# Last state sums as row scalings and bf16 adds, and C2 summed by adding DMAs, in a two-branch sequence kernel

## The chip, the cores and the metric

The kernel runs on one core of one Trainium2 chip. The metric is the device time of one execution in microseconds (us); lower is better. The program's own order is written out by hand, step by step, so every engine works through a fixed queue.

## The reference

Two branches read x of 2048 rows by 512 columns, and a gate for each row mixes them. Branch a is a diagonal state space model with 512 complex states, branch b is linear attention with 32 heads of 16 and softmax features.

```python
    h = jnp.zeros_like(Bu[:, 0, :])
    for t in range(L):                       # branch a: 2048 steps
        h = Lam_bar[None, :] * h + Bu[:, t, :]
        hs.append(h)
    y = 2.0 * jnp.einsum("blp,dp->bld", hseq, Cmat).real + x * Dskip[None, None, :]
...
    phi_q = jnp.concatenate([_softmax(pq, axis=-1), _softmax(-pq, axis=-1)], axis=-1)   # branch b
    kv = jnp.einsum("bhsf,bhsd->bhfd", phi_k, v)
    num = jnp.einsum("bhqf,bhfd->bhqd", phi_q, kv)
    den = jnp.einsum("bhqf,bhf->bhq", phi_q, z)[..., None] + 1e-6
    o = num / den                            # then heads joined, @ wo
...
    g = _sigmoid((x * gate_w).sum(-1, keepdims=True))
    return g * a + (1 - g) * b
```

## The kernel before

**States.** The 2048 time steps are stored as eight residues r = 0 to 7 of 256 cells. The complex states stand as eight groups m of 64 states, real parts in one half of the 128 partitions and imaginary parts in the other. `LS[:, m, u]` holds the states of the residues u and u + 4 for u = 0, 1, 2, and `HH[:, m]` those of the residues 3 and 7. Steps `b` and `g` (L645 to L681) compute the inputs of the states and local recurrences on TensorE, `z` a scan over cells, `sa`, `sb` and `H` bring the states of HH up to date.

What is then missing is, for each m and each u, the product of a complex number per state with the states before. It can be added in three ways, and `UNITS` (L61) says which is used where: u = 1 first (names h..), then u = 0 (e..), and last u = 2 (d..), which needs the finished u = 1.

- `by_pe` (second letter p): a matmul with a diagonal matrix into PSUM, then a DVE add from PSUM.
- `by_row` (second letter k): two row scalings into one of four slots in `CT` (real part times the states; imaginary part times the states with both partition halves swapped), then two bf16 adds on DVE. The swapped states lie in `HHs`, which is `CS` used again; `st_X` or `st_X2` copies them there by DMA on SyncE's queue.
- `by_dma` (second letter d): the same two scalings for two m at once, then two DMAs from GpSimd's queue that add into LS.

**C2.** Steps `c0` to `c3` scale the transposed C matrices in `CT` by complex numbers into `CS` and `CT`, and `C` (L696) brings CS by four DMAs into the layout of `C2`, against which the states are multiplied in `y`. Since CT is the scratch of the scalings above and CS that of the swapped states, both must have been read before these start.

**Attention.** `k`, `v`, `q` project tiles of 128 rows. `x`, `n`, `e`, `s` and, for queries, `X`, `N`, `E`, `S` make the softmax features of a group of tiles: largest and smallest value, differences, exponentials on ScalarE (ACT), then sums, and for queries transposes by DMA. `a` accumulates the keys' sums, `Y` brings them from PSUM. `o` makes the output of a tile of rows (a matmul, logarithm and exponential `ld` and `rd` on ACT, the DVE product `on`, L891); `O` transposes `on` of two tiles by DMA on SyncE's queue into `oT`.

**Output.** `y` (L847) accumulates states times C2 in a PSUM bank for each of sixteen tiles; `t` adds `oT` times Wo into the same bank and scales by the gate. Tiles 8 to 11 have a residual `xd` (step `u`) that is added then. The tiles 12 to 15 belong to the residues 2 and 6 and so need all of u = 2. `R` stores two tiles; the last tile is cut into 384 and 128 columns.

**Order.** Each step is a generator, and the string `ORDER` lists in which order they are advanced; `name@banks` gives PSUM banks and `name:D` puts the piece on VectorE (DVE) instead of ACT. All instructions of an engine stand in this order in its queue, and an engine whose next instruction waits does nothing else.

Of the kernel before, what the change touches and what calls it, by code (L numbers as in the profile page):

```python
# [23 lines left out]
ORDER = """
Z@0 Lk Lk Z Z Z B Z Z B Z Z Z Lx Z Z W01@2 Z W00@3 Z B Z W00 Z B W01 W10@1 W00 Lx B W10:D W11@4 Lx W01 Z f0@2 f1@5
T1@1 W11 T0@4 f0:D f1 Lv T1 f2@3 f3@0 Lx Lx T0:D f2 V@2 V k1@5 P k0@4 f3:D P Lx P2 P k0 P2 P2 U P2 k1 P2 U P3 P4 k0
k1 U k2@2 P3 P4 k3@1 n0 v0@5 P4 x0 k5@6 k2 v1@2 Lb Lq n0 i x0 P2 k7@0 v3@4 i V2@3 k3 x0 v0 k5 i n0 i k9@1 x0 v1 i i
Lq x0 n0 Lb k7 M n0 k8@7 k4@0 M k6@2 n1 M Lx w2@6 x1 w0@5 V2 v6@3 x0z Lx n1 x1 v3 n1 L Da Lx Lb Lb x1 Lb Da Lb e0 n1
k4 w3@4 k6 k9 w3 x1 w0 x1 v6 k10@0 n1 k10 s0 x2 k11@2 s0 w1@4 k8 M2 e1 k13@1 k15@3 w1 Db x2 k15 b11@7 U x2 b10@5 k11
b01@0 b20@4 n2 x2 Lc n2 b10 x2 n2 s0 w2 n2 M2 s0 k13 b00@3 n2 M2 g01@5 Da Db x3 g10@1 b30@6 s0 b01 b20 s0 Lc e2 Db  # L30
s1 b31@4 g10 g30@0 n3 b30 s0 c1:D x3 b00 g00@3 s1 g30 k12@6 c0:D b31 g00 g01 k14@2 e2 b11 a0@74 g00 gw a0 g01 g10 n3
q1@1 s1 b21@3 n3 x3 s1 Da s1 x3 g30 v2@0 c0:D k12 n3 s1 q3@6 k14 q0@2 g01 s2 x3 n3 s2 q1 q1 b21 Lc c0:D q2@3 n4
g11@1 x4 e3 g11 g11 q3 v2 g31@0 g01 s1 x4 q3 g20@6 g31 q0 q0 a1 q2 n4 s2 x4 e3 g31 g20 c0 g11 g01 n4 c2 g01 g31 a1
g01 g20 s2 g21@2 x4 q2 g11 s3 Lc g21 c2 g21 g11 s2 v5@3 g01 g21 c1 v5 g31 g21 s2 x4 v4@6 g21 s3 c2:D g31 s3 b40@3
g01 g11 v4 g21 n4 s3 g31 g21 s3 g31 v7@5 b50@6 b40 g21 g31 n4 g11 s2 q6@3 X0 N0 G0 c1 g21 s2 X0 g11 a2 q4@2 c2 g31
q7@0 c1 g11 q6 N0 b50 z0@6 c3 Lo z0 b70@1 v7 a2 q4 s3 z0 q4 q5@5 q7 a2 e4 q6 s3 q7 b70 q5 X0 e4 N0 z0 a2 c3 X0 b71@3
z0 g40@6 X0 b61@1 N0 z0@0 b71 g50@2 b61 g50 g50 q5 z0 z0 b51@5 X1 c3 v10@0 g40 s4 b60@3 z0 sa0@2 g70@1 b51 g61@5 N0
X1 b60 g71@3 s4 g71 g70 v10 g51@0 c3 sa0 X1 g40 sb0@2 Ld s4 s3 N1 g60@6 sb0 N1 s4 g51 g61 g51 N1 E0 E0 C g60 C g70
g51 S0 v11@2 s4 G1 N1 G0 v8@1 g60 Ld S0 g51 H1@6 g61 v11 s4 v8 X1 S0 b41@2 v9@1 g51 H1 S0 s4 hd1 C g51 s4 a3 S0 g71
v9 g41@6 a3 b41 g41 H0@2 g41 a3 a3 hd1 G0 g71 g51 C S0 g71 g61 g41 G1 S0 g71 g61 H0 g41 XX0 g41 q9@2 g61 g71 hd0 G1  # L40
g51 g51 g61 g71 g41 g61 q10@1 X1 g61 XX0 g41 N1 q9 g71 g41 g61 q8@0 g71 g41 S0 hd1 z1@6 q8 q10 z1 S0 z1 q11@3 q9 q11
v13@6 z1 q10 E1 q8 E1 z1 v12@0 XX0 z1@1 X2 N2 v14@2 q14@5 v13 q11 v12 z1 z1 X2 XX0 v15@1 N2 q12@3 z1 v15 hd0 v14 S0
S0 N2 hd1 hd1 hd0 hd1 q14 S1 a4 N2 S1 X2 sa1@0 a4 S1 sa1 a4 q12 a4 sb1@6 S1 q13@0 Y Y sb1 S1 hd0 q15@7 Y X2 H2@6 Y
o0@1 q14 G2 S1 END q15 X2 XX1 y1@5 q15 hd0 q13 q12 S1 o0 o1@3 H3@7 N2 y1 H3 o1 H2 hd0 o3@6 XX1 XX1 o0 q13 o0 o1 E2
E2 o1 N3 S1 XX1 y3@0 hk4 S1 o2@1 y2@4 y0@3 y2 O0 o2 y0 S1 y0 S2 o3 X3 o2 hk6 y1 o3 hk4 hk7 o2 t1 t0 y3 o3 hk7 hk6
y4@1 y2 S2 hk4 hk5 O1 t0 S2 o5@6 X3 S2 y3 hk4 hk7 S2 N3 t1 X3 S1 o4@2 S2 y6@5 hk5 X3 t2 S2 o5 ek0 hk5 hk7 R0 S2 o4
o5 o4 ek0 t3 hk5 hk6 t2 o4 ek3 ek3 o5 t3 o6@2 S2 N3 S2 hk6 X3 N3 o6 o7@6 y5@4 ek0 o7 o6 N3 o6 O2 o7 o7 ek2 ek1 y5 y4
y6 S2 dp5@0 ek1 y4 ek3 y5 dp6@2 o8@6 dp6 dp5 y6 E3 t4 ek2 Ld o9@2 o8 ek0 y7@0 o9 y7 ek2 ek1 o8 t5 o8 o9 ek2 o9 ek1
ek4:D E3 o10@6 t4 y7 o10 O3 o11@2 ek5 S3 t7 ek3 o10 t6 ek6 o11 ek4 o11 O4 y10@1 o10 S3 G2 dp1@6 ek5:D y11@7 t6 t7 t5
o11 ek5 S3 O5 ek7 ek6 ek4 ek5 ek7 S3 dp0@2 ek6 R2 ek7 ek4 y9@0 ek6 ek7 S3 dp7@4 y8@3 dp2@5 S3 dp2 y10 y8 dp3@5 t8  # L50
y11 S3 R1 S3 dp7 dp4@4 G2 dp1 u8 S3 S3 S3 t11 t8 G3 dp0 t10 y9 t9 o13@2 dp3 o13 o12@5 o12 u9 dp4 t9 R3 y14@4 y12@0
u10 o12 G3 y14 o12 o13 o15@5 o13 o15 y12 o15 o14@2 t10 o14 G3 y12 o14 u11 o15 y13@1 O6 y13 t11 y15@56 y15 y13 t12
t13 R4 R5 o14 O7 y14 t14 O8 t12 t13 R6 y15 t14:D R7 t15 t15 t15 R8 t15:D R8
"""
# [20 lines left out]
def kernel(  # L75
# [610 lines left out]
    def st_c(j):  # L686
        scaled(CS[:, 1, j], CT[:, 0, j], csp[:, 1, j:j + 1])
        yield
        scaled(CS[:, 0, j], CT[:, 1, j], csp[:, 2, j:j + 1])
# [3 lines left out]
        VT(out=CS[:, :, j], in0=CS[:, :, j], in1=CT[:, :, j], op=ALU.add)
# [307 lines left out]
```

## Time and profile before

| | us |
|---|---|
| median of 3 runs (lowest, highest) | 151.49 (151.43, 152.28) |
| the profiled execution, its own time | 151.96 |
| its span | 150.2 |
| TensorE (PE) busy | 140.9 |
| VectorE (DVE) busy | 135.1 |
| ScalarE (ACT) busy | 121.9 |
| GpSimd (POOL) busy | 21.4 |

The span is the time from the first to the last instruction of the profiled execution; what lies around it is 1.8 us. The granted TensorE clock was 0.996 over the span. Busy times of different engines overlap. A line such as L735 is that line of the kernel before; in the changed kernel lines are one higher up to L692, and a few higher behind.

### The profile page before, as it was taken

The numbers are of one execution on the slowest core, as the hardware profiler recorded it, in microseconds if no ns is written. First come the engines' busy times: TensorE is split into PE (matmuls) and PEld (weight loads), VectorE is DVE, ScalarE is ACT, GpSimd is POOL, SyncE is SP. The second block draws the span as 40 slices with busy tenths as digits, with TensorE's granted clock in tenths as the row PEclk, the third lists the DMA queues.
The fourth block names the chain that finished last, engine by engine and source line by source line (L and its number), as shares of the span: only waits on it lengthen the run. The fifth ranks groups of instructions, "written<-read, shape, count | busy, mean of one in ns | idle before, by whom it ended". The sixth has DMA issues, their size and how long they took to land.

```text
span 150.2 us, 2835 instructions
## 1 busy us (share of the span) xinstructions
PE 140.9 (94%) x986; PEld 75.2 (50%) x986; DVE 135.1 (90%) x332; ACT 121.9 (81%) x241; POOL 21.4 (14%) x47
## 2 busy tenths in 40 slices
...
GB/s 120 237 265 178 143 230 232 166 180 238 20 0 0 0 0 4 2 0 105 244 74 94 183 142 70 175 186 181 229 181 166 156 65 212 128 214 77 201 82 72
DMA packets 54110, 19.73 MB, mean 131 GB/s; under 512 B 44496, under 2 KB 54096, under 8 KB 54096
## 3 DMA queue, kind: packets, MB, share of 16 engines
...
q14 instruction: 7, 0.06, 0.2%
...
## 4 chain that ended last, share of the span: by engine, by line
PE 55%; DVE 24%; SPq 10%; DMA 7%; issue 1%; ACT 0%; DVEq 0%
PE PS L516 12%; PE PS L860 9%; PE PS L648 9%; PE PS L643 9%; PE PS L916 6%; SPq L236 5%; DMA xT<-in_A_x_dram 4%; DVE on L891 3%; DVE sm L566 3%; SPq L249 3%; DMA oT<-on 3%; PE PS L660 2%; DVE EE L577 2%; DVE EE L616 2%; DVE HH L735 2%; DVE EE L583 2%
## 5 line engine op out<-in xcount | busy, mean ns | idle before, releaser
L516 PE MATMUL PS<-WKV,xT 128*128 128x480 bf16 (+1 forms) x128 | 29.6, 373 | 1.7 <-DMA xT<-in_A_x_dram 1.7
L589 ACT ACTIVATE EE<-EE 128x2048 bf16<-128x2048 bf16 x16 | 30.7, 1944 | 0.0
L516 PEld LDWEIGHTS <-xT 128*128 128x128 bf16 x192 | 18.3, 99 | 20.0 <-DMA xT<-in_A_x_dram 1.8
L860 PE MATMUL PS<-C,LS 128*128 128x512 bf16 (+1 forms) x104 | 23.0, 363 | 0.0
L135 ACT CAST Xq<-PS 128x480 bf16<-128x480 f32 x32 | 17.6, 584 | 1.7 <-PE PS L516 1.7
L916 PE MATMUL PS<-Wo,oT 128*128 128x512 bf16 (+2 forms) x68 | 15.6, 367 | 0.3 <-DMA oT<-on 0.3
L643 PE MATMUL PS<-xT,BT 128*128 128x512 bf16 x64 | 15.7, 379 | 0.0
L648 PE MATMUL PS<-xT,BT 128*128 128x512 bf16 x64 | 15.6, 379 | 0.0
L516 PE MATMUL PS<-Wq,xT 128*128 128x481 bf16 x64 | 15.0, 367 | 0.0
L135 ACT CAST LS<-PS 128x512 bf16<-128x512 f32 x24 | 14.1, 630 | 0.9 <-PE PS L648 0.7
L860 PEld LDWEIGHTS <-LS 128*128 128x128 bf16 x104 | 9.5, 98 | 9.7
L684 POOL DMA_DIRECT2D LS<-CT x4 | 4.9, 1226 | 62.2 <-ACT HH L135 49.6
L922 ACT ACTIVATE ot<-PS,G 128x512 bf16<-128x512 f32 (+1 forms) x11 | 7.2, 670 | 5.8 <-PE PS L916 5.7
L882 ACT ACTIVATE ld<-PS 128x32 f32<-128x32 f32 x16 | 2.8, 197 | 10.2 <-PE PS L877 7.6
L465 ACT ACTIVATE CT<-HH,dgs 128x512 bf16<-128x512 bf16 x15 | 10.7, 718 | 0.2 <-DVE HH L735 0.2
L891 DVE TENSOR_TENSOR on<-PS,rd 128x512 bf16<-128x512 f32 x16 | 10.8, 710 | 0.0
L577 DVE TENSOR_TENSOR EE<-Xq,mx 128x2048 bf16<-128x2048 bf16 (+1 forms) x9 | 10.0, 1107 | 0.8 <-PE PS L633 0.8
L465 ACT ACTIVATE CT<-CS,nsn 128x512 bf16<-128x512 bf16 x15 | 10.5, 725 | 0.0
L583 DVE TENSOR_TENSOR EE<-mn,Xq 128x2048 bf16<-128x2048 bf16 (+1 forms) x9 | 10.0, 1112 | 0.0
L566 DVE TENSOR_TENSOR sm<-EE 128x2048 bf16<-128x2048 bf16 (+1 forms) x9 | 10.0, 1107 | 0.0
L135 ACT CAST vx<-PS 128x512 bf16<-128x512 f32 x16 | 9.9, 633 | 0.1
L604 DVE TENSOR_TENSOR EE<-EE,rc 128x2048 bf16<-128x2048 bf16 x8 | 9.7, 1219 | 0.1
...
## 6 DMA issues: line engine op xcount, KB each, us to landing
out_dram<-ot SPq DMA_DIRECT2D x7, 256.0 KB, 2.4
C<-CS SPq DMA_DIRECT2D x4, 256.0 KB, 4.0
CS<-HH SPq DMA_DIRECT2D x8, 128.0 KB, 3.5
LS<-CT POOLq DMA_DIRECT2D x4, 256.0 KB, 4.5
...
```

What stands on the lines that cost most here:

```text
L135: nc.scalar.copy(out=out_ap, in_=in_ap)
L465: nc.scalar.mul(out=out_ap, in_=in_ap, mul=s_)
L516: MM(out=pt[:], lhsT=xT[:, kt, ti * P:(ti + 1) * P], rhs=W[:, kt, 0:pt.shape[-1]], start=(kt == 0), stop=(kt == KT - 1))
L566: VT(out=dst, in0=cur[:, :, :, 0:n, :], in1=cur[:, :, :, n:2 * n, :], op=op)
L577: VT(out=half(EE, 0), in0=X5, in1=live["mx", p].to_broadcast([P, L, 8, Dh, 4]), op=ALU.subtract)
L583: VT(out=half(live["EE", p], 1), in0=live["mn", p].to_broadcast([P, L, 8, Dh, 4]), in1=X5, op=ALU.subtract)
L589: aexp(out=EE[:, l_:l_ + 2], in_=EE[:, l_:l_ + 2], func=ACT.Exp)
L643: MM(out=pt[:], lhsT=BT[:, m, kt, :], rhs=cells(kt, r), start=(kt == 0), stop=False, skip_group_check=True)
L648: MM(out=pb[:], lhsT=BT[:, m, kt, :], rhs=cells(kt, 2 * pr), start=(kt == 0), stop=(kt == KT - 1))
L860: MM(out=py[:], lhsT=hs[m], rhs=C2[:, m, c:c + w], start=(m == 0), stop=False)
L891: VT(out=live["on", g_][:, u], in0=pn[:, :, :, 0:Dh], in1=rd[:].unsqueeze(3).to_broadcast([P, 2, 16, Dh]), op=ALU.mult)
L916: MM(out=py[:], lhsT=oT[:, g, :], rhs=Wo[:, g, c:c + w], start=False, stop=(g == HG - 1))
```

## The change

The names dp0 to dp7 in `UNITS` become dk0 to dk7: the sums of u = 2 are made by `by_row` instead of `by_pe`. With that the step XX2 comes in, two DMAs that bring the partition halves of `LS[:, :, 1]` swapped into HHs. In `st_c` the DVE sum of CS and CT goes; a new step `A` adds CT into C2 by four adding DMAs on GpSimd's queue after `C` has stored CS there.

```diff
-UNITS = (... (2, 'dp0', 0), (2, 'dp1', 0), (2, 'dp2', 0), (2, 'dp3', 0), (2, 'dp4', 0), (2, 'dp5', 0), (2, 'dp6', 0), (2, 'dp7', 0))
+UNITS = (... (2, 'dk0', 0), (2, 'dk1', 0), (2, 'dk2', 0), (2, 'dk3', 0), (2, 'dk4', 0), (2, 'dk5', 0), (2, 'dk6', 0), (2, 'dk7', 0))
...
         scaled(CT[:, :, j], CT[:, :, j], csp[:, 0, j:j + 1])
         yield
-        VT(out=CS[:, :, j], in0=CS[:, :, j], in1=CT[:, :, j], op=ALU.add)
-        yield
...
+    def st_A():
+        for q, pq_ in ((0, 0), (1, 1), (0, 1), (1, 0)):
+            add_by_dma(C2[q * HS:(q + 1) * HS, pq_::2], CT[pq_ * HS:(pq_ + 1) * HS, 1 - q])
+            yield
```

The list of steps is another one from the first line to the last. Its end, from the transfers XX2 on:

```diff
-o7 o6 N3 o6 O2 o7 o7 ek2 ek1 y5 y4 y6 S2 dp5@0 ek1 y4 ek3 y5 dp6@2 o8@6 dp6 dp5 y6 E3 t4 ek2 Ld o9@2 o8 ek0 y7@0
-...
-t13 R4 R5 o14 O7 y14 t14 O8 t12 t13 R6 y15 t14:D R7 t15 t15 t15 R8 t15:D R8
+o11 ek6 o11 y11 S3 y10@4 G2 S3 y10 o10 S3 XX2 t4 S3 y9@3 o11 y8@6 dk0 S3 S3 XX2 dk2:D O4 dk1 dk1 y8 dk0 y9 t5 R3 dk2
+t8 t9 S3 dk0 O5 dk3 dk1 S3 dk5 dk2 dk0 dk4 dk2 G3 t10 dk6 dk4 G2 S3 dk6 dk5:D t11 dk3 o12@1 u10 S3 dk3 dk4 dk7 dk5
+o12 o12 y12@7 dk6 dk7 dk4 t10 y13@4 dk6 dk7 o12 o13@0 y14@2 o13 o13 dk5 dk7 u11 o13 y14 G3 y12 R2 u8 o14@0 t11 t8
+y14 y13 y13 o14 y12 o14 o14 u9 o15@5 O6 G3 y15@01 R5 y15 o15 O7 o15 t9 t13 t12 o15 R4 t14 y15 O8 t12 t14 t15 t13:D
+t15 R6 t15 R7 t15:D R8 R8
```

At its start the loads Wv (`Lv`) stand ahead of the first x transpose (`Lx`), the loads of B (`Lb`) ahead of the last four, and the transposes of Wq (`Lq`) behind all but one of them; the projections v0 and v2 stand ahead of k0.

More of the change, by code (lines that the diff above doesn't have):

```diff
@@ L24 @@
 ORDER = """
[L25 to L49, printed above, removed]
@@ L50 @@
-o11 ek5 S3 O5 ek7 ek6 ek4 ek5 ek7 S3 dp0@2 ek6 R2 ek7 ek4 y9@0 ek6 ek7 S3 dp7@4 y8@3 dp2@5 S3 dp2 y10 y8 dp3@5 t8
-y11 S3 R1 S3 dp7 dp4@4 G2 dp1 u8 S3 S3 S3 t11 t8 G3 dp0 t10 y9 t9 o13@2 dp3 o13 o12@5 o12 u9 dp4 t9 R3 y14@4 y12@0
-u10 o12 G3 y14 o12 o13 o15@5 o13 o15 y12 o15 o14@2 t10 o14 G3 y12 o14 u11 o15 y13@1 O6 y13 t11 y15@56 y15 y13 t12
-t13 R4 R5 o14 O7 y14 t14 O8 t12 t13 R6 y15 t14:D R7 t15 t15 t15 R8 t15:D R8
+Z@0 Lk Z Z Z Lk B Z Z B Z W01@1 Lx W00@2 B B Z Z Z Z Z B Lx Z W10@3 W11@4 W00 W10 Lv W01 T0@3 Lx Z W11 f2@4 f3@5
@@ new lines @@
+T1@6 W01 f2 W00:D Lx T1 V@1 Lx Z f1@2 f0@7 T0:D V P Z v0@1 Lb f0 v2@0 P f1 f3 P2 P2 P2 k0@2 P2 V2@7 P P2 k1@6 P2 P4
+Lb Lx P4 k1 k0 P3 P3 k3@5 k4@4 P4 k1 k0 i k6@2 i k4 V2 k5@6 k2@4 i k3 M i k7@5 x0 n0 v1@7 Lx v6@3 x0 n0 gw v0 n0 x0
+i x0 k6 M n0 k2 M x0 i U n0 k5 x1 Lx n1 x1 k9@6 n1 k8@4 v1 v3@7 x1 k10@2 k11@1 Lb n1 x1 Lb Lq Lq k7 n1 v2 x1 L b00@0
+n1 k9 M2 b10@6 Da Lx e0 v3 b30@7 n2 x2 x2 n2 x2 k10 b00 s0 g30@0 k11 b20@1 Db e1 n2 b31@2 s0 Db b30 U g00@7 k8 v6 n2
+b20 k12@1 x2 s0 Lc Da g30 x2 s0 M2 n2 b31 U k13@2 g20@3 x3 b10 g20 s0 n3 s1 w2@6 b11@4 e2 U g00 Da x3 n3 k12 k15@1
@@ new lines @@
+s1 n3 x0z e2 v7@5 k13 w1@2 Lc s1 s0 w2:D w0@6 k15 k14@1 g30 g20 b11 w1 w3@3 M2 w0 Lb s1 b01@0 s1 x3 s2 b01 s1 x3
+b21@2 s0 s2 w3 a0@64 a0 Lc g31@0 g00 b21 s2 Db n3 s2 s2 q1@3 q0@2 Da k14 q1 x3 n3 c1 x4 Lc q1 g31 q3@1 c0:D v7 c3
+g31 c3:D v4@7 q0 g01@3 s2 c2:D n4 x4 q3 g21@5 g01 c2:D n4 Lb q3 q2@1 g01 q0 g10@2 v4 n4 s1 x4 c0:D e3 a1 s2 g01 g31
+g01 x4 g21 q2 e3 C g21 a1 g10 g31 q4@7 q2 g10 n4 g31 b40@1 g11@2 c2:D q4 a2 g21 g31 s2 b40 g11 g21 s3 g11 x4 g01 g31
+c3:D g31 q4 g21 g11 g01 Lo X0 n4 N0 b50@1 c1 v5@7 g21 g31 g11 g01 b50 g11 g01 v5 c1:D q10@1 g50@0 a2 a2 a2 X0 g21 G0
@@ new lines @@
+g11 s3 N0 e4 s3 g11 X0 g01 N0 g21 X0 g21 q7@7 q10 g11 s3 g11 G0 b61@3 z0@2 b51@5 q10 z0 z0 g50 q5@2 X0 q7 e4 z0 b61
+q5 g50 s4 b51 s3 b70@1 q6@3 v8@0 N0 q5 z0 z0@5 s4 b60@2 z0 c0 q6 q7 q11@7 z0 N0 X1 g51@5 s4 b60 q6 s3 g60@2 z0 b71@3
+q11 g60 X1 b70 g51 E0 v9@1 v8 g51 sa0@0 C s3 b71 g70@3 E0 q11 X1 N1 s3 s4 g70 sa0 v9 b41@7 S0 g70 a3 g51 A sb0@1
+v10@0 g61@3 g61 A sb0 g60 a3 g61 b41 Ld S0 H1@7 v11@1 H0@2 N1 G1 v10 S0 N1 Ld C S0 g40@0 C G1 s4 A H1 s4 S0 a3 G0
+g40 A g71@7 g71 S0 s4 XX0 v11 H0 g71 X1 hd1 g51 g61 a3 hd1 g41@2 g40 hd0 s4 g41 N1 g51 g71 S0 g41 g51 g61 g71 g41
@@ new lines @@
+g51 g61 q8@0 hd1 g71 g61 g61 g41 X1 XX0 S0 q8 g41 g51 N1 g71 q9@1 g61 g71 S0 XX0 g51 q9 g41 g41:D g71 g41 g71 g61:D
+q8 G1 g41 z1@5 q9 X2 z1 X2 XX0 N2 S0 v14@2 v13@1 v15@7 v12@0 z1 E1 E1 X2 v13 z1 N2 v14 v12 z1 z1@5 N2 z1 Ld S0 X2
+v15 hd1 hd0 N2 q12@3 q14@1 S1 q12 a4 a4 z1 a4 S1 a4 z1 S1 Y q13@7 sa1@5 S1 X2 sa1 q12 hd1 q14 Y q15@0 q15 Y Y sb1@2
+hd0 o3@5 o2@3 hd1 hd0 END sb1 S1 hd0 S1 q15 N2 H2@2 o3 q13 y2@0 XX1 o2 q13 S1 H3@7 o2 o3 H2 y3@2 E2 E2 H3 o2 o3 y1@7
+o0@3 y2 hd0 o1@5 X3 y3 y1 o0 XX1 G2 S1 hk7 o1 X3 o0 hk4 S2 XX1 o0 o1 XX1 y1 y4@3 S2 y2 o1 S2 O1 S1 q14 hk5 hk6 hk7
@@ new lines @@
+y0@4 hk5 S2 t2 hk4 hk4 S1 t2 O0 hk7 y0 y3 t3 hk5 N3 S2 hk4 hk6 o5@0 o4@5 X3 S2 y0 S1 hk7 ek0 hk5 S2 hk6 t3 ek1 o4 t0
+t1 y5@2 o5 S2 o4 hk6 ek0 N3 S2 o5 ek1 t0 o4 t1 N3 y4 ek1 y4 ek3 o5 o6@5 N3 ek2:D ek1 o6 S2 ek2:D ek3 ek0 o6 ek3 o7@0
+X3 S2 ek2 y7@4 ek3 y6@7 o6 o7 o7 ek5 o7 y6 ek7 ek2 y6 o9@5 o8@0 ek0 X3 y7 ek5 o9 N3 ek4:D y5 ek7 o8 ek6:D y7 ek6 ek7
+O2 ek5 y5 t5 o8 ek4 O3 t7 o8 o10@0 R0 o9 R1 E3 ek7 E3 t6 ek5 o10 ek4 t6 o9 t7 ek6 t4 y11@5 o10 o11@6 ek4 dk3 dk1 S3
+o11 ek6 o11 y11 S3 y10@4 G2 S3 y10 o10 S3 XX2 t4 S3 y9@3 o11 y8@6 dk0 S3 S3 XX2 dk2:D O4 dk1 dk1 y8 dk0 y9 t5 R3 dk2
@@ L60 @@
 ZB = 2
-UNITS = ((1, 'hd0', 1), (1, 'hd1', 1), (1, 'hk4', 1), (1, 'hk5', 1), (1, 'hk6', 1), (1, 'hk7', 1), (0, 'ek0', 0), (0, 'ek1', 0), (0, 'ek2', 0), (0, 'ek3', 0), (0, 'ek4', 0), (0, 'ek5', 0), (0, 'ek6', 0), (0, 'ek7', 0), (2, 'dp0', 0), (2, 'dp1', 0), (2, 'dp2', 0), (2, 'dp3', 0), (2, 'dp4', 0), (2, 'dp5', 0), (2, 'dp6', 0), (2, 'dp7', 0))
+UNITS = ((1, 'hd0', 1), (1, 'hd1', 1), (1, 'hk4', 1), (1, 'hk5', 1), (1, 'hk6', 1), (1, 'hk7', 1), (0, 'ek0', 0), (0, 'ek1', 0), (0, 'ek2', 0), (0, 'ek3', 0), (0, 'ek4', 0), (0, 'ek5', 0), (0, 'ek6', 0), (0, 'ek7', 0), (2, 'dk0', 0), (2, 'dk1', 0), (2, 'dk2', 0), (2, 'dk3', 0), (2, 'dk4', 0), (2, 'dk5', 0), (2, 'dk6', 0), (2, 'dk7', 0))
 XLOADS = ((2, 2), (4, 2), (6, 2), (8, 2), (10, 2), (12, 2), (14, 2))
```

2 lines of the change are left out of this document (1 added, 1 removed).

## The prediction

> **What bounds the kernel now.** I read the page's busy times first, then the busy time by stretches of ten microseconds, then the chain that ended last, and then the instructions of VectorE (DVE), ScalarE (ACT) and SyncE's queue in order of time near the end.
>
> ```profile
> PE 140.9 (94%) x986; PEld 75.2 (50%) x986; DVE 135.1 (90%) x332; ACT 121.9 (81%) x241; POOL 21.4 (14%) x47
> ```
> ```profile
> 110.00:120.00 10.00, 9.70 (x88) 5.32 (x84) 10.00 (x21) 9.54 (x20) 0.00 (x0) 1.00 0.97 169
> 120.00:130.00 10.00, 9.76 (x46) 4.46 (x47) 10.00 (x25) 6.47 (x15) 0.00 (x0) 1.00 0.56 120
> 130.00:140.00 10.00, 10.00 (x78) 5.22 (x77) 9.37 (x17) 1.97 (x8) 0.00 (x0) 1.00 0.79 170
> 140.00:150.20 10.20, 6.10 (x50) 3.68 (x47) 1.10 (x2) 1.96 (x3) 0.00 (x0) 0.94 0.37 103
> ```
>
> The columns are the stretch, its length, then PE, PEld, DVE, ACT and POOL busy with their counts. Three engines are full at once up to about 127 us. ACT stops first, DVE next, and PE alone fills the end. The page's 94% for PE flatters it, because matmuls overlap; DVE, at 90% with its idle time at the two ends, is the engine with no room. The last instructions show how the end comes about:
>
> ```profile
> 115.99 4.20 DMA oT<-on
> 120.24 1.90 PE PS L916 x8
> 122.14 0.86 PE PS L860 x4
> 123.00 0.21 PE PS L811
> ```
> ```profile
> 145.91 0.58 ACT ot L922
> ```
> ```profile
> 126.86 0.19 ACT L818 ACTIVATE G<-nge 128x4 f32<-128x4 f32 x1
> 134.09 0.45 ACT L882 ACTIVATE ld<-PS 128x32 f32<-128x32 f32 x2 [7.04 <-PE PS L877]
> ```
> ```profile
> 136.43 0.74 DVE L920 SCALAR_TENSOR_TENSOR ot<-PS,G,xd 128x512 bf16<-128x512 f32 x1
> 137.09 0.17 DVE L822 RECIPROCAL G<-G 128x4 f32<-128x4 f32 x1
> 137.17 0.73 DVE L896 SCALAR_TENSOR_TENSOR xd<-WKV,G,Drow 128x512 f32<-128x512 bf16 x1
> 137.81 0.69 DVE L891 TENSOR_TENSOR on<-PS,rd 128x512 bf16<-128x512 f32 x1
> 138.41 0.74 DVE L920 SCALAR_TENSOR_TENSOR ot<-PS,G,xd 128x512 bf16<-128x512 f32 x1
> 139.07 0.68 DVE L891 TENSOR_TENSOR on<-PS,rd 128x512 bf16<-128x512 f32 x1
> ```
>
> The chain from 120.24 to 145.91 is matmuls without a gap. ACT has done its bulk at 127.05 and then waits 7.04 us. DVE's last product `on` ends at 139.75, and the last output scaling on ACT starts 6.16 us after that. So a change pays by shortening DVE's queue, or by shortening those 6.16 us; ACT may grow at the end, and nowhere else.
>
> **The change, part by part.** I cost an instruction on a full engine by the distance between starts, not by its duration, since neighbours overlap by about 0.1 us.
>
> ```profile
> 115.00 1.32 DVE L735 TENSOR_TENSOR LS<-PS,LS 128x512 bf16<-128x512 f32 x2
> 116.20 0.46 DVE L806 TENSOR_TENSOR LS<-CT 128x512 bf16<-128x512 bf16 x1
> 116.53 0.80 DVE L804 TENSOR_TENSOR CT<-CT,LS 128x512 bf16<-128x512 bf16 x2
> 117.20 0.73 DVE L891 TENSOR_TENSOR on<-PS,rd 128x512 bf16<-128x512 f32 x1
> ```
> ```profile
> 122.06 0.40 DVE L467 TENSOR_SCALAR CT<-CS,nsn 128x512 bf16<-128x512 bf16 x1
> 122.33 0.73 DVE L891 TENSOR_TENSOR on<-PS,rd 128x512 bf16<-128x512 f32 x1
> ```
> ```profile
> 45.73 0.69 DVE L693 TENSOR_TENSOR CS<-CS,CT 128x1024 bf16<-128x1024 bf16 x1
> 46.34 0.29 DVE L566 TENSOR_TENSOR mn<-mn 128x256 bf16<-128x256 bf16 x1
> ```
>
> *DVE.* Removed are the eight adds out of PSUM of dp0 to dp7 (1.20 / 2 = 0.60 each, 4.80) and the four sums of CS and CT in st_c (0.61 each, 2.44). Added are sixteen bf16 adds of dk0 to dk7 (0.33 each, 5.34). The new list also marks other steps for DVE: four more row scalings (six for two; 0.27 each, 1.08), two more 512-wide scalings and one more 1024-wide one in st_c (0.27 each and at most 0.54; I take 0.9 in all), one fold evacuation less (I take the 0.57 of a 480-wide evacuation, between the 0.60 of an add out of PSUM and nothing) and two 64-wide evacuations more (at most 0.3). Sum: -4.80 -2.44 +5.34 +1.08 +0.9 -0.57 +0.3 = -0.2 us. DVE's queue is as long as before: the two halves of the change cancel on the engine that counts.
>
> *PE.* Eight 512-wide matmuls go, 0.21 each as the row of L811 shows: 1.7 us less, most of it in the closing run from 120.24 on, and nothing is added.
>
> *ACT.*
>
> ```profile
> 84.35 3.71 ACT L589 ACTIVATE EE<-EE 128x2048 bf16<-128x2048 bf16 x2
> 87.96 1.55 ACT L135 CAST vx<-PS 128x512 bf16<-128x512 f32 x3
> ```
> ```profile
> 119.65 0.72 ACT L465 ACTIVATE CT<-HH,dgs 128x512 bf16<-128x512 bf16 x1
> 120.26 0.32 ACT L885 ACTIVATE rd<-ld,nge 128x32 f32<-128x32 f32 x1
> ```
> ```profile
> L465 ACT ACTIVATE CS<-CT,csp 128x512 bf16<-128x512 bf16 x5 | 3.8, 761 | 0.0
> L465 ACT ACTIVATE CT<-CT,csp 128x1024 bf16<-128x1024 bf16 x2 | 2.4, 1200 | 0.0
> ```
>
> Fourteen of the sixteen dk scalings run here at 0.61: 8.5. Away go two ek scalings (1.2), two CS scalings and one CT scaling in st_c (their means less the 0.1 of overlap: 2.4), one evacuation more comes than goes (0.5), and two 64-wide ones leave (0.35). Net +5.05 us, so ACT's bulk would end near 132 instead of 127, where before it waited. That is hidden as long as the last dk add is due after about 132.
>
> *The copies.* XX2 puts two more transfers of 256 KB on SyncE's queue, behind the oT transposes of O2 and O3 and the stores R0 and R1, and the swapped dk scalings wait for them; queued behind those on ACT are the remaining dk scalings, the `ld` and `rd` of o12 to o15, and so DVE's last products. A puts four adding transfers on POOL's queue.
>
> ```profile
> C<-CS SPq DMA_DIRECT2D x4, 256.0 KB, 4.0
> CS<-HH SPq DMA_DIRECT2D x8, 128.0 KB, 3.5
> LS<-CT POOLq DMA_DIRECT2D x4, 256.0 KB, 4.5
> ```
> ```profile
> oT<-on SPq DMA_TRANSPOSE x9, 3.1
> ```
> ```profile
> L684 POOL DMA_DIRECT2D LS<-CT x4: 1190/1196/1322, 78.8 to 95.1; - x4
> ```
>
> XX2 can issue once the last ek scaling is done and lands some 5 us later (3.5 and 4.0 us for the copies of 128 and 256 KB, and the second issue). In the new order of ACT, between the last ek scaling and the first swapped dk scaling stand E3's two exponentials (1.80 each, by the starts 84.35 and 87.96), three output scalings, three plain dk scalings and small ones: some 8 us. So I cost XX2 at nothing; bounds are nothing and, if SyncE is as late as at 115.99 with a transpose that took 4.20, 2 us. For A: between the last step of c0 on ACT and hd1's first scaling, which overwrites what A reads, the new order has twenty ACT instructions, among them two exponentials and thirteen evacuations (0.47 each, 87.96 with its three): 10.8 us. Three issues of 1.2 and a landing of 4.5 are 8.1. A costs nothing too, with 2.7 us to spare; without that cover ACT would stand still. C itself no longer waits for the sums and starts sooner.
> The Trainium skill (DMA: Bandwidth & Descriptors, SWDGE vs HWDGE vs iDMA) says that GpSimd writes the rings of its DMAs in state from which DVE's two-port modes lock it out. The four POOL issues of this trace took 1190 to 1322 ns beside a DVE that was nearly full, so it does not show such a hold-up; by the rule A's transfers would start one after another and the time would be that of rival 3.
>
> *The start.* The new list loads Wv before the x transposes and B before Wq, and runs v0 and v2 ahead of k0. PE's one long early wait is this:
>
> ```profile
> 22.57 1.79 PE L516 MATMUL PS<-WKV,xT 128*128 128x480 bf16 x8 [1.65 <-DMA xT<-in_A_x_dram]
> ```
>
> The transposes for k10 and k11 now stand ahead of both Wq transposes, so up to 1.65 us of this wait may go. DVE is full meanwhile, so I count nothing; bounds are a gain of 1.65 and, should the earlier B loads delay k8 and k9 instead, a loss of 1.
>
> *The end.* After the last dk add, DVE still has three `on` (0.60), three `xd` and three `ot` (0.66) and two small ones (0.08) before o15's product is done: 5.9 us. PE has from there two dozen 512-wide matmuls (0.215 each, 5.2), y15 and t15 (2.6), sixteen 128-wide ones and two o steps (1.4): 9.1 us. With DVE's last product at 139.55 the last dk add is at 133.6, PE can be done at 142.8, and o15's way is longer: transpose 3.1, a queue step of 0.1, the 384-wide matmuls 0.67, which is 3.9 after `on` instead of 6.16. That is **the gain: 2.3 us**, because the 1.7 us of diagonal products no longer lie in PE's closing run, and PE no longer ends later than the oT transpose allows.
>
> *Given back.* In the new order DVE has, after the last of N3 (the differences whose exponentials E3 takes), 25 bf16 adds (8.3), eight `on` (4.8), four `xd` and four `ot` (5.3), four row scalings (1.1), G3's sums and products (3.8, an estimate from the 0.33 of a 512-wide and the 0.61 of a 1024-wide add) and small ones (0.3): 23.6 us. So E3 can start at 116.0 and ends at 119.6, and 12.6 us of ACT work (fourteen dk scalings 8.5, four output scalings at the 0.58 of the last one, small ones 1.8) lead to 132.2. Twice ACT must wait for DVE in this stage, for `smf` and for `dl`: 1.1 us by the same sums. With two adds behind the last scaling (0.7) the last dk add ends at 134.0, 0.4 late. For the four slots of CT that dk4 to dk7 must wait for I add 0.3; bounds are nothing and 5.4, below.
>
> Sum against the profiled execution of 151.96 us: -0.2 -2.3 +0.4 +0.3 = -1.8, 150.2. That execution is 0.47 over the median of 151.49, so against the median: **149.7 us**, 1.2% less. A measurement of this kernel tells about 1% from no change, which puts the bounds at 149.98 and 153.0.
>
> **The rivals.** (1) *The gain is given back as idle time of DVE.* In the list of before, DVE stood idle for only about 2 us between 8 and 139.75; a list searched anew need not be as dense. For: three full engines, with ACT's queue 5 us longer. Against: DVE's load is unchanged. With 1 to 3 us more idle it ends at 150.7 to 152.7; I take 151.5. (2) *Slower: the slots.* by_row has four slots for eight m, so dk4 to dk7 start only after the second adds of dk0 to dk3 on DVE. If every reuse costs a full trip (0.71 for the scaling, 0.46 for each of two adds, 0.6 for an `on` in front: 2.2 for each of four, against 8.4 us for the stage without waits, 4.9 of them for the first four), the stage lasts 13.8, 5.4 more, and the time is 155.1. It decides the sign from 3.3 us of such waits on. For: in the new order o12's product and two `xd` stand among these adds. Against: dk1 and dk3 run ahead, so the trips overlap. (3) *A lands late and holds hd1 on ACT.* If the four adds go one after another at the 4.5 of their landing, they need 18 us where 10.8 are covered: 7.2 us on a full ACT, 156.9; it would take issues much longer than the 1.2 us of the rows, or adds that don't overlap, and the trace of before shows neither. The rule named with A would bring this about. (4) *The start's 1.65 us count as well:* 148.0.
>
> **How the numbers follow.** Forecast 0.46 (its own range 148.8 to 150.6, six parts in seven of it under 149.98), rival 1 0.26, rival 2 0.18, rival 3 0.05, rival 4 0.05. Faster: 0.40 + 0.05 = 0.45. Within 1%: 0.06 + 0.26 = 0.32. Slower: 0.23. The range takes in rival 4, the forecast, rival 1 and the lower part of rival 2: 148.0 to 153.4.
>
> **What would show it.** Right: DVE full to about 139.5 with its last `on` there; ACT's bulk ending near 132; the last output scaling on ACT starting about 4 us after the last `on`, with the oT transpose as its releaser; PE with no wait for the adds of the dk steps beyond a few tenths. Wrong: waits of ACT for DVE adds at the dk scalings of over 3 us in sum (rival 2); a wait of ACT's hd1 scaling for LS or C transfers (rival 3); SyncE holding XX2 so that the swapped scalings wait; DVE idle for more than 3 us between 10 and 139 (rival 1). If DVE's last product comes well before 139, my price list for DVE is wrong.

## The result, and the profile after

The changed kernel takes 149.98 us (median of 4 runs, 149.85 to 150.24) beside 151.55 for the kernel before (151.43 to 152.28): ratio 0.9889, 95% interval 0.9866 to 0.9912, 1.1% less. The forecast was 149.7 with a range of 148.0 to 153.4. Run once more, it had 150.33 (ratio 0.9883, 0.9847 to 0.9920). The profiled execution of after has 149.94 us and a span of 148.2; that of before had 151.96 and 150.2.

First the page's busy times, then the last stretches of 10 us (stretch, length, PE, PEld, DVE, ACT, POOL busy, granted clock, DMA share, GB/s):

```profile
PE 139.1 (94%) x962; PEld 73.8 (50%) x978; DVE 135.5 (91%) x344; ACT 127.8 (86%) x249; POOL 27.3 (18%) x51
```
```profile
110.00:120.00 10.00, 9.52 (x88) 5.33 (x88) 10.00 (x25) 9.73 (x20) 0.00 (x0) 1.00 1.08 216
120.00:130.00 10.00, 9.89 (x53) 4.47 (x52) 10.00 (x26) 9.82 (x20) 0.00 (x0) 1.00 1.00 182
130.00:140.00 10.00, 9.86 (x86) 5.46 (x86) 9.94 (x22) 5.47 (x15) 0.00 (x0) 1.00 0.73 161
140.00:150.20 10.20, 4.66 (x33) 2.60 (x32) 1.94 (x4) 1.96 (x3) 0.00 (x0) 0.96 0.37 103
```

ACT now works to 134 instead of 127, DVE has as much to do as before, and only PE has less. Take PE's account alone: before, 150.2 of span less 140.9 busy leaves 9.3 us in which PE stood idle; after, 148.2 less 139.1 leaves 9.1. By this account PE's shorter work is nearly the whole gain of this execution. The account says where the time went, and not what allowed it: before_thin below takes 1.4 us off PE in the old list and gains nothing. The end of the chain that ended last, and the last rows of ACT and DVE:

```profile
126.91 5.27 DMA phT<-EE
132.71 1.67 PE PS L864 x7
134.64 2.59 PE PS L864 x12
139.28 1.75 PE PS L864 x16
141.07 2.54 PE PS L920 x11
```
```profile
132.23 0.43 PE L881 MATMUL PS<-KVm,phT 128*128 128x68 bf16 x8
```
```profile
133.24 0.71 ACT L466 ACTIVATE CT<-CS,nsn 128x512 bf16<-128x512 bf16 x1
144.52 0.58 ACT L926 ACTIVATE ot<-PS,G 128x384 bf16<-128x384 f32 x1 [0.18 <-PE PS L920]
```
```profile
133.98 0.75 DVE L810 TENSOR_TENSOR LS<-CT 128x512 bf16<-128x512 bf16 x2
140.16 0.68 DVE L895 TENSOR_TENSOR on<-PS,rd 128x512 bf16<-128x512 f32 x1
```

The transposes of the last query features (phT) are done at 132.18, the product o12 that reads them starts at 132.23, and from there PE works to the end. The two rows for the kernel before, on PE and in SyncE's queue:

```profile
133.63 0.67 PE L877 MATMUL PS<-KVm,phT 128*128 128x68 bf16 x16
```
```profile
127.91 4.81 SPq L620 DMA_TRANSPOSE phT<-EE  x2
```

Before, o12 started at 133.63, 0.9 us behind the end of its transposes and 12.28 us ahead of the last scaling on ACT (145.91). Now it is 12.29 us ahead of it (144.52). So the question is what lets o12 start 1.4 us earlier.

### The profile page after: what moved, and what is told of

Same layout as the page of the kernel before. It is cut to its first block, busy times and chain, and to the rows that moved or that the text cites. A ratio compares the mean times of both kernels' runs of the same rounds, so it can differ in the third digit from the quotient of the medians.

```text
span 148.2 us, 2857 instructions
## 1 busy us (share of the span) xinstructions
PE 139.1 (94%) x962; PEld 73.8 (50%) x978; DVE 135.5 (91%) x344; ACT 127.8 (86%) x249; POOL 27.3 (18%) x51
## 4 chain that ended last, share of the span: by engine, by line
PE 60%; DVE 22%; ACT 6%; DMA 5%; issue 4%; DVEq 0%; SPq 0%
PE PS L517 23%; PE PS L644 9%; PE PS L649 9%; PE PS L864 5%; DMA phT<-EE 4%; DVE on L895 3%; DVE sm L567 3%; ACT EE L590 2%; PE PS L920 2%; PE PS L634 2%; DVE LS L810 2%; DVE CT L808 2%; DVE mn L567 2%; DVE HH L739 2%; DVE mx L567 2%
## 5 line engine op out<-in xcount | busy, mean ns | idle before, releaser
L517 PE MATMUL PS<-WKV,xT 128*128 128x480 bf16 (+1 forms) x125 | 28.7, 372 | 0.2
L864 PE MATMUL PS<-C,LS 128*128 128x512 bf16 (+1 forms) x100 | 21.8, 362 | 0.3
L136 ACT CAST Xq<-PS 128x480 bf16<-128x480 f32 x32 | 18.4, 586 | 1.2 <-PE PS L517 1.2
L644 PE MATMUL PS<-xT,BT 128*128 128x512 bf16 x64 | 16.1, 379 | 0.1
L649 PE MATMUL PS<-xT,BT 128*128 128x512 bf16 x64 | 15.8, 380 | 0.1
L517 PE MATMUL PS<-Wq,xT 128*128 128x481 bf16 x64 | 15.5, 368 | 0.1
L466 ACT ACTIVATE CT<-CS,nsn 128x512 bf16<-128x512 bf16 x22 | 15.2, 715 | 0.0
L920 PE MATMUL PS<-Wo,oT 128*128 128x512 bf16 (+2 forms) x67 | 15.1, 366 | 0.1
L136 ACT CAST vx<-PS 128x512 bf16<-128x512 f32 x16 | 9.3, 604 | 0.5 <-PE PS L517 0.4
L920 PEld LDWEIGHTS <-oT 128*128 128x128 bf16 x68 | 6.2, 98 | 6.5 <-DMA oT<-on 0.5
L649 PEld LDWEIGHTS <-BT 128*128 128x128 bf16 x64 | 6.1, 99 | 6.4
L644 PEld LDWEIGHTS <-BT 128*128 128x128 bf16 x64 | 6.1, 98 | 6.4
```

Source lines behind the costliest of these rows:

```text
L136: nc.scalar.copy(out=out_ap, in_=in_ap)
L466: nc.scalar.mul(out=out_ap, in_=in_ap, mul=s_)
L517: MM(out=pt[:], lhsT=xT[:, kt, ti * P:(ti + 1) * P], rhs=W[:, kt, 0:pt.shape[-1]], start=(kt == 0), stop=(kt == KT - 1))
L644: MM(out=pt[:], lhsT=BT[:, m, kt, :], rhs=cells(kt, r), start=(kt == 0), stop=False, skip_group_check=True)
L649: MM(out=pb[:], lhsT=BT[:, m, kt, :], rhs=cells(kt, 2 * pr), start=(kt == 0), stop=(kt == KT - 1))
L864: MM(out=py[:], lhsT=hs[m], rhs=C2[:, m, c:c + w], start=(m == 0), stop=False)
```

## The experiments

The table holds five times from the profiled execution of each kernel: DVE's first product of the parameters (ssm_par from vec), the first differences of N3 on DVE (before's list has them at another place), o12 on PE, the last output scaling on ACT, and the last time less the first. The ratio is that of the timed runs to the kernel before.

| kernel | first product | N3 | o12 | last scaling | last less first | ratio (95%) |
|---|---|---|---|---|---|---|
| before | 8.83 | 110.73 | 133.63 | 145.91 | 137.1 | 1 |
| after | 9.05 | 114.95 | 132.23 | 144.52 | 135.5 | 0.9889 (0.9866, 0.9912) |
| again | 10.05 | 115.94 | 132.97 | 145.26 | 135.2 | 0.9883 (0.9847, 0.9920) |
| c2_dve | 9.04 | 116.76 | 134.08 | 146.37 | 137.3 | 1.0055 (1.0029, 1.0081) |
| dp_back | 9.03 | 114.91 | 133.69 | 146.78 | 137.8 | 1.0075 (1.0040, 1.0111) |
| pe_refill | 9.98 | 116.19 | 134.96 | 147.24 | 137.3 | 0.9992 (0.9964, 1.0021) |
| before_A | 8.96 | 112.33 | 134.74 | 147.01 | 138.1 | 1.0066 (1.0043, 1.0089) |
| before_thin | 8.94 | 110.76 | 132.92 | 145.28 | 136.3 | 0.9999 (0.9986, 1.0011) |
| no_dk | 9.34 | 115.21 | 132.24 | 144.52 | 135.2 | 0.9906 (0.9880, 0.9932) |
| start | 9.19 | 115.31 | 132.34 | 144.64 | 135.5 | 0.9925 (0.9893, 0.9957) |
| start_v | 10.25 | 116.56 | 133.69 | 145.98 | 135.7 | 0.9952 (0.9925, 0.9979) |
| no_ek | 8.89 | 112.47 | 132.16 | 144.44 | 135.6 | 0.9917 (0.9889, 0.9945) |
| pe_less | 9.05 | 114.96 | 132.42 | 144.71 | 135.7 | 0.9919 (0.9888, 0.9949) |
| no_ek_less | 10.63 | 114.24 | 132.76 | 145.78 | 135.2 | 0.9896 (0.9862, 0.9930) |

The theory at the outset was the prediction's: DVE's queue is full and sets the end, PE follows it. Its rivals were that only one half of the change gains, or that PE alone sets the end.

**c2_dve: the sums of C2 back on DVE.**

```diff
         scaled(CT[:, :, j], CT[:, :, j], csp[:, 0, j:j + 1])
         yield
+        VT(out=CS[:, :, j], in0=CS[:, :, j], in1=CT[:, :, j], op=ALU.add)
+        yield
...
 in the list: the sum behind the third step of each c; the four A become the four C, the early C go
```

> Base: the changed kernel, 149.98. Undone: the adding DMAs A; the four sums of CS and CT are DVE adds again (0.61 us each), C stores after them. Theory of the queues (DVE is full from 13 to 140 us, and its length is passed on to the end): DVE is 2.4 us longer, 152.4 (151.6 to 152.6). Rival (ACT and PE set the pace where these sums stand, at 45 to 65 us, and DVE has room for them): 150.0 to 150.4.

152.77 us, ratio 1.0055: 2.5 us more than after (0.0166 of 151.5), as the theory of the queues had it. The table shows how it runs through: N3 1.81 later, o12 1.85, the end 1.85. Rows of DVE and PE of c2_dve, in order of time, and PE's sum of waits from 48 to 72 us (us in all, times, longest):

```profile
53.82 0.69 DVE L693 TENSOR_TENSOR CS<-CS,CT 128x1024 bf16<-128x1024 bf16 x1
54.43 0.15 DVE L550 TENSOR_SCALAR nge<-PS 128x1 f32<-128x1 f32 x1
```
```profile
54.63 1.02 PE L516 MATMUL PS<-WKV,xT 128*128 128x512 bf16 x4 [1.02 <-DVE nge L550]
```
```profile
PE PS L516 <- DVE nge L550: 1.3, 2, 1.0
```

The sum stands ahead of the small `nge`, which frees the PSUM bank that PE wants, and PE waits 1.3 us, where after has no such wait and PE stands idle for 0.16 us in all in the same stretch. At this place a late DVE makes PE late, and nothing behind makes it good.

**before_A: the adding DMAs alone, in the list of before.** The edit is that of the change in `st_c` and its step A; in the old list the four C now stand together behind the second step of c3, the last of the c steps, and the four A behind its third.

> Base: the kernel before, 151.5. Done alone: C2 is summed by four adding DMAs on GpSimd's queue, and the four DVE sums go; list otherwise as before. Theory of the queues: DVE is 2.4 us shorter; ACT, full at the same time with 2.4 us idle between 40 and 127, passes on only part, 150.0 (149.2 to 150.6). Rival (PE's closing run sets the end of the kernel before, whatever DVE does): 151.3 to 151.6.

152.90 us, ratio 1.0066, slower than before by 1.0: neither theory nor rival had that. From its GpSimd and ACT rows, and its SyncE queue:

```profile
67.33 3.22 POOL L684 DMA_DIRECT2D C<-CT  x3 [38.08 <-DMA C<-CS]
```
```profile
77.61 0.72 ACT L465 ACTIVATE CT<-HH,dgs 128x512 bf16<-128x512 bf16 x1 [1.92 <-DMA C<-CT]
```
```profile
72.04 10.29 SPq L777 DMA_DIRECT2D CS<-HH  x4
```

In the old order A is issued 3 us later than in the new one (64.34). ACT waits 1.92 us for A's transfers before hd1, and SyncE's four copies of the swapped states, which start 3.6 us earlier than before's (75.63, over 5.33 us), end 1.4 us later. This is the prediction's rival 3, in the other list: a landing, not an issue, holds hd1. So A alone, put into the old list like this, costs more than it saves; in the new list, which moves the c steps ahead, ACT did not wait for it.

**dp_back: u = 2 by diagonal products again, in the list of after.**

```diff
-UNITS = (... (2, 'dk0', 0), ... (2, 'dk7', 0))
+UNITS = (... (2, 'dp0', 0), ... (2, 'dp7', 0))
...
 in the list: a matmul and an add of each dp stand at places where dk steps stood; XX2 goes
```

> Base: the changed kernel, 149.98. Undone: dk0 to dk7; the sums of u = 2 are matmuls with the diagonal and DVE adds out of PSUM again, at the places in the list where the dk steps stood, and XX2 goes. Theory of the queues: DVE is 1.1 us shorter, PE's closing run 1.7 longer, so about 0.6 slower, 150.6 (150.0 to 151.2). Rival 1 (the row scalings are the gain): 151.3 or more. Rival 2 (the gain comes from C2 and from the list, and the dk steps cost): 149.0 to 149.6.

153.13 us, ratio 1.0075, 2.8 us more than after: above the theory's range and in that of rival 1. The places of the dp steps are mine, not searched, so this is an upper bound of what the row scalings are worth. The waits from 119 us on:

```profile
DVE LS L738 <- PE PS L814: 2.2, 2, 1.6
PE PS L863 <- DVE ot L923: 0.3, 1, 0.3
```

DVE now waits 2.2 us for the products, and o12 starts 1.46 later. Undone singly, the two halves cost 2.5 and 2.8 us, together more than the whole gain of 1.6: they are not two savings that add. Both undone at once in the new list was not run, so how much of the gain the new order would bring without the change stays open.

**pe_refill: 1.7 us of empty matmuls put back on PE, ahead of o12, in after.**

```diff
+    def st_Q():
+        pq_ = bank([P, 512], F32, "pq_")
+        while True:
+            MM(out=pq_[:], lhsT=Sw[:], rhs=C2[:, 0, :], start=True, stop=True)
+            yield
...
 in the list: eight Q at the places of eight dk steps
```

> Base: the changed kernel, 149.98. Added: eight 512-wide matmuls whose result nobody reads, at the places in PE's order where the dk steps stand, 1.7 us of PE ahead of o12. Theory (PE's closing run is tight again in the changed kernel, with 0.3 to 0.6 us of waits ahead of o12): 151.2 (150.9 to 151.6). Rival (the dk chain on ACT and DVE alone sets the end, PE has room until the last dk add): 150.0 to 150.3.

151.82 us, ratio 0.9992, 1.6 more than after and a little above the theory's range: the eight matmuls cost their own 1.7 us, almost in full, and the whole gain is gone. Its o12:

```profile
134.96 0.42 PE L886 MATMUL PS<-KVm,phT 128*128 128x68 bf16 x8
```

The row before it on SyncE, the last two phT transposes (128.16, 4.83 us long), had ended at 132.99. Here o12 waits for PE's own queue.

**before_thin: the diagonal products of before 64 columns wide.**

```diff
-        MM(out=pd[:], lhsT=dg[:, k, m, :], rhs=prevs(m) if u < 2 else LS[:, m, 1], start=True, stop=True)
+        MM(out=pd[:, 0:64], lhsT=dg[:, k, m, :], rhs=LS[:, m, 1, 0:64], start=True, stop=True)
```

> Base: the kernel before at 151.49 us. Its eight diagonal products of u = 2 are made only 64 columns wide (the rest of each product is left out; the DVE adds from PSUM stay 512 wide), so PE loses 8 x (0.21 - 0.06) = 1.2 us, most of it in its closing run, and DVE and ACT lose nothing. Theory of the prediction (these products lay in PE's closing run, which set the end after DVE's last `on`): the tail of 6.16 us after `on` becomes about 5, time about 150.3, ratio 0.992. Rival (DVE's queue alone bounds; the tail shortened for other reasons, such as the new order of PE): 151.4 to 151.5, ratio 0.999 to 1.

151.81 us, ratio 0.9999 (0.9986 to 1.0011): no gain, though PE has 1.4 us less (139.5 against 140.9). SyncE's and PE's rows of its profiled execution say why no more than 0.7 could come:

```profile
127.91 4.83 SPq L620 DMA_TRANSPOSE phT<-EE  x2
```
```profile
132.92 0.68 PE L877 MATMUL PS<-KVm,phT 128*128 128x68 bf16 x16
```

SyncE ends the phT transposes at 132.74, where before had them at 132.72 too, and o12 follows at 132.92. In the old list the transposes end 0.9 us before PE's own queue reaches o12, so with less PE work alone o12 meets them at once. That one execution is 0.6 us shorter within its span and the timed runs are not: that difference stays open.

**no_dk: all sums of u = 2 left out of after.** The dk steps and XX2 are struck from the list.

> Base: the changed kernel at 149.98 us, ratio 0.9889. All sums of u = 2 (dk0 to dk7) and the copies XX2 are left out: DVE loses sixteen adds and two scalings (5.34 + 0.54 = 5.9 us), ACT fourteen scalings (8.5), PE nothing. Theory (DVE's queue sets the end, PE's last tiles follow it): limited by what else lies in the way, the feature transposes of the last group and PE's run from o12 on, which in the changed kernel starts 0.4 us after the transposes land; the time falls by 1 to 3 us, 147 to 149, ratio 0.970 to 0.983. If DVE alone decided, by 5.9: 144.1, ratio 0.951. Rival (PE's closing run is the bound and the dk steps are wholly hidden): 149.7 to 150.0, ratio 0.988.

150.23 us, ratio 0.9906 against 0.9889: no gain, to within some 0.4 us by the intervals. The stretches of no_dk, its last `on`, and a part of the chain that ended last:

```profile
120.00:130.00 10.00, 9.94 (x54) 4.47 (x52) 8.04 (x18) 5.21 (x12) 0.00 (x0) 1.00 0.59 103
130.00:140.00 10.00, 10.00 (x89) 5.59 (x87) 6.74 (x12) 2.08 (x8) 0.00 (x0) 1.00 0.74 161
```
```profile
140.16 0.68 DVE L893 TENSOR_TENSOR on<-PS,rd 128x512 bf16<-128x512 f32 x1
```
```profile
121.64 1.13 DVE sm L565
123.17 5.79 PE PS L862 x26
128.95 3.45 PE PS L918 x16
```

Between 120 and 140 us DVE has 5.2 us less to do than in after and ACT 8.0, and DVE's last `on` stands at 140.16, to the hundredth where it stood with all sixteen adds. This fells the theory that DVE's queue sets the end with the dk adds. It does not fell it for the time ahead of them: from 105 us on the chain of no_dk runs over DVE up to 123 us, to the last add of u = 0, and over PE from there, and in c2_dve the four sums on DVE were paid in full.

**start and start_v: V and f2 placed anew in the first 10 us.** In after, DVE waits 1.29 us for the product V.

```diff
-f2@4 f3@5 T1@6 W01 f2 W00:D Lx T1 V@1 Lx Z f1@2 f0@7 T0:D V P
+f2@4 f3@5 T1@6 V@7 W01 W00:D Lx T1 Lx Z f1@2 T0:D f2:D V f0@7 P
```

start_v leaves f2 on ACT.

> Base: the changed kernel at 149.98 us, ratio to the kernel before 0.9889. Same work; at the start the small product V of the parameters uses the free bank 7 and stands before the second part of W01 and f2, and f2's evacuation is moved from ACT to DVE. Theory (DVE stands still at the start, 1.29 us before its first parameter step and 0.28 at the second, and since it is full from there to its last `on` all of it is paid): the 0.6 us evacuation fills part of the hole, the parameters start about 1.3 us earlier, the time falls by 0.7 to 1.3 us to about 149.0, ratio 0.982. Rival (the queue has slack further on that takes it up, or ACT and PE decide the first 10 us): 149.9 to 150.0, ratio 0.988 to 0.989. If f2's evacuation on DVE costs what the hole gives back: 150.0 or a little above.

> Base: the changed kernel at 149.98 us, ratio 0.9889. As the run `start`, but f2's evacuation stays on ACT: only the product V is moved ahead, on bank 7. Theory (the hole of 1.29 us on DVE is paid in full): V's matmul at about 7.0 instead of 8.26, DVE's parameter steps 0.9 to 1.3 us earlier, time 148.8 to 149.3, ratio 0.981 to 0.984. Rival (ACT's casts or PE decide the start, so that the steps behind the parameters wait for them instead): 149.9, ratio 0.988.

Ratios 0.9925 and 0.9952: no gain, so neither is a better version. Whether they lose is not shown; the runs of start alone that count in its ratio lie between 149.5 and 151.68 us. PE's first matmuls of start_v name what was missed:

```profile
6.16 1.46 PE L319 MATMUL PS<-ident,CS 128*128 128x128 bf16 x12 [1.07 <-DMA CS<-in_B_wqkv_dram]
```

The first tile of Wqkv landed 4.8 us after its issue here and 4.7 in start, 3.6 in the profile of after. The hole that I moved V into is behind that load, so the early V was not tested apart from it.

**again, no_ek, pe_less, no_ek_less: after once more, and with work left out ahead of o12.** no_ek strikes ek0 to ek7 from the list; pe_less makes eight products of y8 and y9 narrow:

```diff
+                w_ = 64 if n in (8, 9) and m > 3 else w
-                MM(out=py[:], lhsT=hs[m], rhs=C2[:, m, c:c + w], start=(m == 0), stop=False)
+                MM(out=py[:, 0:w_], lhsT=hs[m], rhs=C2[:, m, c:c + w_], start=(m == 0), stop=False)
```

> The changed kernel itself, once more, beside the next three: the runs so far that edit it scattered by up to 2 us, with the first tile of Wqkv landing 3.6 to 4.8 us after its issue. Theory (the scatter belongs to the changed order, whose first products wait for that load): the changed kernel scatters too, by 1 us or more, its median 150 to 151, ratio to the kernel before 0.989 to 0.994. Rival (the scatter came with the edits): within 0.3 us of 150.2, ratio 0.987 to 0.991.

> Base: the run `again`. All sums of u = 0 (ek0 to ek7) are left out: DVE loses sixteen bf16 adds and a few scalings (about 6 us), ACT about a dozen scalings (about 7.5 us), most of it before and around the last differences of N3; PE loses nothing. Theory (from o12 on PE runs 12.3 us without a gap to the end, and o12 waits for two things that came within 0.3 us of one another, the last feature transposes and PE's own queue ahead of it): the transposes land 3 to 5 us earlier, but PE can use only its own waits between 110 and 132, 0.3 + 0.5 us: -0.3 to -1.0 us. Rival (DVE's and ACT's queues alone set the end): -4 to -6 us.

> Base: the run `again`. Eight of the products of y8 and y9, which stand in PE's queue ahead of o12, are made 64 columns wide instead of 512 (the rest of each is left out): PE has 8 x (0.215 - 0.03) = 1.5 us less, DVE and ACT nothing. Theory (the last feature transposes land just before o12, so they take over as the bound): 0 to -0.4 us. Rival (PE's queue alone sets the end): -1.5 us.

> Base: the run `again`. Both edits together: the sums of u = 0 left out, and eight products of y8 and y9 64 wide. Theory (two bounds close together, so that only both edits move the end): o12 is ready 1.5 us earlier for PE and its transposes 3 to 5 us earlier, the time falls by 1.7 to 2.5 us, clearly more than the sum of the two single runs. Rival (one bound only): the same as the larger of the two single runs.

The run again scattered by 1.7 us (149.24 to 150.95), as its theory had it, though its ratio of 0.9883 lies in the rival's range. Against this 0.9883 the three have 0.9917, 0.9919 and 0.9896: nothing gained, by one edit or by both, with intervals of about 0.5 us either way. The rivals of -4 to -6 us and of -1.5 us are out. So is my theory of two bounds, since both together should have brought 1.7 to 2.5. First pe_less, waits on PE ahead of o12 and at it; then no_ek; then pieces of the last stretch of the chain of no_ek_less:

```profile
129.84 1.90 PE L921 MATMUL PS<-Wo,oT 128*128 128x512 bf16 x8 [0.91 <-DMA oT<-on]
132.42 0.43 PE L882 MATMUL PS<-KVm,phT 128*128 128x68 bf16 x8 [0.68 <-DMA phT<-EE]
```
```profile
116.68 1.04 PE L918 MATMUL PS<-Wo,oT 128*128 128x512 bf16 x4 [0.29 <-DMA oT<-on]
118.69 1.04 PE L918 MATMUL PS<-Wo,oT 128*128 128x512 bf16 x4 [0.97 <-DMA oT<-on]
```
```profile
116.67 3.87 DMA oT<-on
120.58 1.04 PE PS L919 x4
121.87 0.88 PE PS L919 x4
129.40 2.46 ACT CT L464 x4
135.89 2.59 PE PS L863 x12
```

With less on PE, PE waits 0.91 us for an oT transpose and 0.68 for phT, 1.6 in all, about what it saved (1.5). With less on DVE and ACT, N3 comes 2.5 us earlier than in after, but PE waits 0.29 and 0.97 for oT. With both, the chain runs over oT and the dk scalings on ACT, and comes back to PE behind o12, at 135.6. So in these executions four chains (PE's queue, phT, oT, and ACT's scalings with the adds behind them) lie so close together that what is saved on one is waited for on another. Work added to PE (pe_refill) or, at an early place, to DVE (c2_dve) costs its full time; the work taken away in no_dk and in these three runs brings nothing.

## Why the prediction was right, point by point

**The time.** Summed were -1.8 us against the profiled execution; it is -2.02 (151.96 to 149.94), and -1.6 by the medians. The sign and the size are right, the size in part by luck: see the tail.

**PE, -1.7.** Measured 140.9 to 139.1 (of after's 978 matmuls sixteen left no record, but no_dk, with all of them, has 139.3). The result needs this term, as pe_refill shows, and it was named as the gain: the diagonal products no longer lie in PE's closing run, which the chain of before shows from 120.24 on. They lay ahead of o12 there; from o12 to the last scaling PE takes 12.3 us in both kernels. By itself the term is not enough: before_thin has it in the old list without a gain.

**What bounds.** Here the working failed, in its first part: "So a change pays by shortening DVE's queue, or by shortening those 6.16 us". DVE's last `on` is late because the products of o14 and o15 on PE are late, not because DVE is full. ACT's `ld` of o15 in after waits for its product:

```profile
139.31 0.20 ACT L886 ACTIVATE ld<-PS 128x32 f32<-128x32 f32 x1 [1.24 <-PE PS L881]
```

no_dk takes 5.2 us from DVE and leaves that `on` where it was. A full engine in the profile's stretches was read as the bound to the end; from about 123 us on it was one of several that the list had filled to the same line. I also had the last phT transposes in no step, though o12 needs them and before's SyncE rows had them end at 132.72, 0.9 us ahead of o12.

**The tail, 6.16 to 3.9.** Measured 3.68 (140.84 to 144.52). The number is right, the mechanism behind it is not. The working had PE done at 142.8 and o15's transpose as the longer way. In after PE never waits for that transpose. From SyncE's queue and PE:

```profile
140.87 1.21 SPq L908 DMA_TRANSPOSE oT<-on  x1
```
```profile
143.67 1.04 PE L920 MATMUL PS<-Wo,oT 128*128 128x384 bf16 x8
```

The transpose lands 2.4 us after its issue, at 143.3, and PE comes to its products only at 143.67, out of work that runs on since 132.23. So PE still sets the end, and that the two ways are 0.4 us apart is luck. The tail is also shorter because its beginning moved: the last `on` ends at 140.84, 1.1 us later than before (139.75), and the sum, with what is given back, had 140.25. So the tail shrank by 2.5 us and the last scaling comes only 1.4 us earlier, and not 1.8. That the span still fell by 2.0 is 0.6 us behind the last scaling (4.29 to 3.68), which no step had. That stretch is 3.7 to 4.3 us over the fourteen profiles, and 4.2 in c2_dve, whose list ends as after's does, so this part is scatter.

**The start.** I counted nothing there. The parameters' first product comes 0.22 us later (8.83 to 9.05), and DVE does less in the first 10 us. First the 10 us of before, then those of after:

```profile
0.00:10.00 10.00, 8.66 (x67) 6.30 (x68) 6.25 (x36) 5.22 (x11) 5.66 (x18) 1.00 0.89 205
```
```profile
0.00:10.00 10.00, 7.76 (x61) 5.36 (x63) 4.82 (x31) 4.97 (x9) 5.70 (x18) 1.00 0.87 200
```

DVE does 1.4 us less in them. How much of the 0.6 us by which the last `on` was late comes from there is not shown. The 1.65 us wait of PE behind the x transposes did go (PE is busy 9.95 us of 20 to 30, before 8.35), and as I had it that is not a gain by itself.

**DVE, -0.2.** Busy 135.1 to 135.5 us with twelve instructions more: the halves do cancel there.

**ACT.** +5.05 foreseen, 121.9 to 127.8 measured, and its bulk ends at 133.95 instead of 132.2. Hidden, as said: the last two dk adds run from 133.98 to 134.73 (foreseen to end at 134.0), and among the dk steps no row of DVE waits.

**The copies.** XX2 is issued at 117.33, and ACT reads the swapped states first at 126.02 without a wait: the cost of nothing was right. The size was not: the two transfers are of 512 KB each, not 256, and took longer than the 4.0 us of the smaller ones:

```profile
CS<-LS SPq DMA_DIRECT2D x2, 512.0 KB, 5.8
```

A was mis-sized too, and cost nothing only just:

```profile
64.34 4.24 POOL L685 DMA_DIRECT2D C<-CT  x4 [26.83 <-DVE ms L733]
```
```profile
L685 POOL DMA_DIRECT2D C<-CT x4: 1118/1639/2258, 64.3 to 66.3; - x4
...
DMA to landing us min/median/max: 5.2/8.3/9.6
```
```profile
76.23 0.72 ACT L466 ACTIVATE CT<-HH,dgs 128x512 bf16<-128x512 bf16 x1
```

I took 4.5 us from issue to landing, from the adding DMAs of before; four together took 5.2 to 9.6. The last issue starts at 66.3; counted from its start the last landing is at 75.9 at the latest, up to 11.6 us after the first issue instead of 8.1. hd1's first scaling on ACT is 11.9 after it, at 76.23. The Trainium skill (DMA: Bandwidth & Descriptors, SWDGE vs HWDGE vs iDMA) has DVE's two-port modes lock GpSimd out of the state in which it writes its DMA rings. From that the prediction had read four landings one after another. The trace does not show that: four landings of 5.2 to 9.6 us fit into 11.6 us, so they overlap, though the issues took up to 2.26 us, longer than the 1.32 at most of before.

**The rivals.** (1) DVE has no more idle time: from 10 to 140 us it is 1.3 us by the stretches, before 2.3. (2) No row of ACT or DVE among the dk steps waits for a slot. (3) Not in this list, but in before_A. (4) The start's gain did not come: DVE's first product of the parameters is 0.22 us later.
